# Weight conversion spread over the feed-forward part of two batches, the first quarter of w_in converted by columns, and first scores kept in PSUM

## The chip, the cores and the metric

The kernel runs on one core of a Trainium2 chip. The metric is the device time of one execution in microseconds. The kernel before takes 824.21 us (median of three runs, 824.08 to 826.26).

## What is computed

For each of 8 batches and 8 heads, 32 packed queries p attend to 576 keys and values of width 64; the result is both key and value for a second attention, by 576 queries q. The 8 heads side by side are the 512 inputs of a feed-forward layer (FFN) with 2048 hidden units and a leaky rectifier.

```python
def sm_attn(qq, kk, vv):
    s = scale * np.matmul(qq, kk.transpose(0, 1, 3, 2))
    s = s - np.max(s, axis=-1, keepdims=True)
    a = np.exp(s)
    a = a / (np.sum(a, axis=-1, keepdims=True) + 1e-09)
    return np.matmul(a, vv)
p_packed = sm_attn(p, k, v)
x = sm_attn(q, p_packed, p_packed)
h = x @ w_in
g = np.maximum(h, 0.0) + alpha * np.minimum(h, 0.0)
out = g @ w_out
```

## The kernel before

**Engines and numbers.** Matmuls in full precision are done in one of two ways. Either both operands are split into a high and a low part and three fast matmuls are summed (hi*hi, hi*lo, lo*hi), or plain f32 operands are used; such a matmul is two instructions in the trace. The weights w_in and w_out arrive as 64-bit floats, and the kernel itself turns them into f32, 128 rows by 512 columns at a time, in `convert` (L103 to L134): a 512 KB load on SP's queue (L112), two ACT instructions (L117, L119), four DVE instructions (L120, L123, L127, L131), then a split into high part (ACT L133) and low part (DVE L134). There are 16 such pieces of w_out and 16 of w_in, 32 **conversions**. The raw data go into buffers that later hold converted w_out pieces (`new_raw`; four of them are kept in turn, `SPARE = 4`).

**Attention.** `attention(b, tp)` treats two of the four head pairs of a batch: scores of the packed queries (`scores`, L189), softmax (L259 to L268), transposes (L294), the packed values (L311 or L316), scores of q (L362, L364), a transpose on DVE (L367), softmax by POOL and DVE over groups of 32 (L369 to L378), and a last transpose into the FFN's input: `a_f` in f32 for batch 0 (L383), `a_h` and `a_l` for the others (L390 to L392). For batches 0 and 1 scores are plain f32 matmuls with 64 output rows (L200), which ACT and DVE copy from PSUM to SBUF (L202, L204).

**Packed weights.** `packed_w` multiplies each piece of w_in with the packed values of a batch (L435 to L437) and so yields `pw`, the FFN's first weights in packed form; on the first use (`fresh`) it converts the piece and writes it split to DRAM (`w_split`, L407); later uses read it back.

**FFN.** The tokens of batch b are the halves k = 2b and 2b+1, of 288 columns each. `first(k, f)` makes 128 hidden units (L468 for batch 0: four instructions; L480 to L482 for the others: six), then ACT L486, DVE L487, ACT L492, DVE L493 make the rectified value, split. `second(k, f)` adds it to four output blocks (L505 to L507: twelve matmuls). One pair (k, f) is an **iteration**; there are 256, the ACT row of L486 marks each one's start, and second runs two iterations behind first. For batch 1 and later `split_pw` first splits pw: high part on DVE (L456), low part on POOL for batch 1 and on DVE from batch 2 on (L458). `order` takes batch 0 in quarters of f, both halves in turn, so that four partial sums are added (`part`, L511, L518); the other batches have all 16 f of one half in a row.

**What sets the order.** `plan` (L574 to L582) says at which iteration which generator (conversions `wo`, `w0`; attention of later batches; packed weights) makes a step, and how often. All w_in pieces for batch 0 (`w0`) and all w_out pieces (`wo`) are converted at one step every second iteration, after a prologue `PRO` of ten steps. A list scheduler then orders each engine's instructions; an engine runs its own list strictly in order, so an instruction that waits holds all behind it, and SP's queue of DMA issues does too.

Of the kernel before, what the change touches and what calls it, by code (L numbers as in the profile page):

```python
# [28 lines left out]
def pack_attention_ffn_kernel(  # L29
# [50 lines left out]

    w_split = dram.tile([NJ, NP, P, 2, 512], F32, name="w_split")


    ident = const.tile([P, P], F32, name="ident")
    make_identity(nc, ident)
    ii = const.tile([P, 64], F32, name="ii")
    nc.gpsimd.tensor_copy(out=ii[0:64], in_=ident[0:64, 0:64])
    nc.gpsimd.tensor_copy(out=ii[64:128], in_=ident[64:128, 64:128])
# [5 lines left out]
    s1f = const.tile([P, NP, 64], F32, name="s1f")  # L94
    p2f = const.tile([P, NP, 64], F32, name="p2f")
    pt0 = const.tile([P, NP, 2, 2, 64], F32R, name="pt0", tag=f"wo{NF - 1}")
    for t in (s1f, p2f, fv(s1), fv(p2), fv(pt0)):
        nc.gpsimd.memset(t, 0.0)
    wo_t = {}

    XF = 1

    def convert(src, raw, place):  # L103
# [8 lines left out]
        nc.sync.dma_start(out=raw, in_=src)  # L112
# [6 lines left out]
        nc.scalar.activation(out=low, in_=u[:, :, 0], func=AF.Copy, scale=2.0**-29)  # L119
        nc.vector.tensor_scalar(  # L120
# [9 lines left out]
        )  # L130
        nc.vector.tensor_tensor(out=bits, in0=bits, in1=low, op=ALU.add)  # L131
# [16 lines left out]
    SPARE = 4  # L148
    left = list(range(NF - 1 - SPARE, NF - 1))

    def load_w_out(f):
# [4 lines left out]
        raw = new_raw(f)  # L156
        convert(w_out[f * P : (f + 1) * P, :], raw, place)
# [31 lines left out]
    def scores(b, pr, st, x, dst, exact):  # L189

        ro = (pr % 2) * 64
        for hf in range(2):
            sl = slice(hf * HS, hf * HS + HS)
            if exact:
                if b == 0:
                    tag = f"acc{(2 * pr + hf) % 4}"
                    ps = ps_a.tile([P, 512], F32, name=tag, tag=tag)
                else:
                    ps = ps_m.tile([P, 512], F32, name="ps_m", tag="m")
                nc.tensor.matmul(ps[:64, :HS], st[:, pr], x[:, sl], start=True, stop=True)  # L200
                if hf or b > 0:
                    nc.scalar.copy(out=dst[ro : ro + 64, sl], in_=ps[0:64, :HS])  # L202
                else:
# [3 lines left out]
            nc.tensor.matmul(ps[:, :HS], st[:, pr], x[0][:, sl], start=True, stop=False)  # L207
# [426 lines left out]
```

## Time and profile before

| | |
|---|---|
| median of three runs | 824.21 us |
| profiled execution, its time | 824.1 us |
| its span, first to last instruction | 822.0 us |
| busy: PE / DVE / ACT / POOL | 782.6 / 607.2 / 486.6 / 206.6 us |
| mean granted clock | 0.985 |

A page of the profile gives the busy time of each engine; the span cut in 40 slices shows it in tenths. Matmuls overlap, so that a PE shown as busy may still be waiting between matmuls; how much it does is told by the number of matmuls in a stretch, and by how long a run of them takes when nothing waits. The timeline gives start and length of single instructions, and the table by stretch gives busy time and, in brackets, the number of instructions.

### The profile page before, as it was taken

How to read it: one execution, taken by the hardware profiler on the slowest of the kernel's cores; microseconds unless marked ns; L12 is line 12 of the kernel's file. 1: busy time of each engine (PE TensorE's matmuls, PEld its weight loads, DVE VectorE, ACT ScalarE, POOL GpSimd, SP SyncE). 2: the span in 40 equal slices, each digit the busy share in tenths (PEclk: the TensorE clock that was granted, in tenths of full speed). 3: DMA queues.
4: the chain of work that ended last, by engine and by line, in shares of the span. 5: the costliest groups of instructions: out<-in, count | busy, mean ns of one | idle time of the engine just before them, and what ended most of it. 6: DMA issues, size and time to landing. Idle time of an engine off the chain costs nothing.

```text
span 822.0 us, 14951 instructions
## 1 busy us (share of the span) xinstructions
PE 782.6 (95%) x5384; PEld 729.1 (89%) x5384; DVE 607.2 (74%) x1303; ACT 486.6 (59%) x1141; POOL 206.6 (25%) x203
## 2 busy tenths in 40 slices
PE   5679998999999999999999999999999999999997
PEld 3357686898799999999999999899999999999997
DVE  4999898975777557899886488987855566666663
ACT  5778866766666775656667765665655533333332
POOL 2100022536667401353362024533210000000000
PEclk9769999999999999999999999999999999999999
DMA  9777855664633561321227621300262000000000
GB/s 301 261 247 234 271 189 197 200 197 160 211 91 109 188 229 44 92 72 60 62 83 237 206 84 52 104 24 15 81 206 84 23 30 2 30 1 30 1 31 29
DMA packets 55385, 97.96 MB, mean 119 GB/s; under 512 B 5136, under 2 KB 32784, under 8 KB 55312
## 3 DMA queue, kind: packets, MB, share of 16 engines
q1 hardware_dynamic: 55312, 97.02, 36.3%
q8 instruction: 42, 0.69, 0.4%
q14 instruction: 31, 0.25, 0.1%
HBM read 79.18 MB, written 17.83 MB: 118 GB/s over the span
## 4 chain that ended last, share of the span: by engine, by line
PE 75%; DVE 13%; ACT 5%; DMA 4%; issue 2%; SPq 1%; POOL 0%; ACTq 0%; DVEq 0%
PE acc L505 15%; PE acc L506 14%; PE acc L507 14%; PE ps_h L480 7%; PE ps_h L482 7%; PE ps_h L481 7%; PE ps_m L435 2%; PE ps_m L436 2%; PE ps_m L437 2%; DMA wraw<-in_w_out 2%; PE ps_h L468 1%; PE ps_m L316 1%; DVE ps_h L487 1%; DVE pwl L458 1%; DVE mag L127 1%
## 5 line engine op out<-in xcount | busy, mean ns | idle before, releaser
L505 PE MATMUL acc<-gh,wo 128*128 128x288 f32 x1024 | 286.8, 300 | 6.8 <-ACT gh L492 4.9
L506 PE MATMUL acc<-gh,wo 128*128 128x288 f32 x1024 | 281.5, 294 | 0.0
L505 PEld LDWEIGHTS acc<-gh,wo 128*128 128x128 f32 x1024 | 192.2, 188 | 18.0 <-ACT gh L492 10.5
L507 PE MATMUL acc<-gl,wo 128*128 128x288 f32 x1024 | 201.0, 301 | 0.0
L506 PEld LDWEIGHTS acc<-gh,wo 128*128 128x128 f32 x1024 | 192.3, 188 | 1.4
L492 ACT CAST gh<-ps_h 128x288 fp32r<-128x288 f32 x256 | 102.2, 399 | 122.0 <-DVE ps_h L487 120.0
L493 DVE TENSOR_TENSOR gl<-ps_h,gh 128x288 fp32r<-128x288 f32 x256 | 115.5, 452 | 73.9 <-ACT gh L492 72.4
L486 ACT ACTIVATE neg<-ps_h 128x288 f32<-128x288 f32 x256 | 105.4, 412 | 104.8 <-PE ps_h L482 98.8
L507 PEld LDWEIGHTS acc<-gl,wo 128*128 128x128 f32 x1024 | 157.8, 188 | 3.6
L487 DVE SCALAR_TENSOR_TENSOR ps_h<-neg,nal,ps_h 128x288 f32<-128x288 f32 x256 | 131.4, 515 | 35.2 <-ACT neg L486 34.2
L480 PE MATMUL ps_h<-a_h,pwh 128*128 128x288 f32 x448 | 133.2, 297 | 1.0 <-DVE gl L493 0.9
L482 PE MATMUL ps_h<-a_h,pwl 128*128 128x288 f32 x448 | 132.1, 296 | 0.7 <-POOL pwl L458 0.7
L481 PE MATMUL ps_h<-a_l,pwh 128*128 128x288 f32 x448 | 131.9, 295 | 0.0
L173 POOL TENSOR_TENSOR xl<-xraw,xh 128x576 fp32r<-128x576 f32 x48 | 70.1, 1461 | 134.4 <-ACT xh L172 124.6
L480 PEld LDWEIGHTS ps_h<-a_h,pwh 128*128 128x128 f32 x448 | 84.1, 188 | 2.9 <-DVE gl L493 1.9
L482 PEld LDWEIGHTS ps_h<-a_h,pwl 128*128 128x128 f32 x448 | 83.9, 188 | 1.3 <-POOL pwl L458 1.1
L481 PEld LDWEIGHTS ps_h<-a_l,pwh 128*128 128x128 f32 x448 | 84.1, 188 | 0.5
L456 DVE CAST pwh<-pw 128x512 fp32r<-128x512 f32 x112 | 55.3, 496 | 35.2 <-PE ps_h L481 33.3
L458 DVE TENSOR_TENSOR pwl<-pw,pwh 128x512 fp32r<-128x512 f32 x96 | 74.7, 778 | 6.6 <-PE ps_h L482 0.8
L443 ACT COPY pw<-ps_m 64x512 f32<-64x512 f32 x112 | 65.0, 581 | 19.2 <-PE ps_m L437 15.3
L275 POOL TENSOR_TENSOR vs<-vraw,vs 128x640 fp32r<-128x640 f32 x24 | 38.6, 1608 | 42.4 <-ACT vs L274 42.4
L210 ACT COPY lo<-ps_m 64x288 f32<-64x288 f32 x96 | 37.8, 395 | 16.9 <-PE ps_m L208 15.4
(112 smaller groups left out, 1021.7 us busy)
## 6 DMA issues: line engine op xcount, KB each, us to landing
w<-w_split SPq DMA_DIRECT2D x64, 512.0 KB, 3.9
xraw<-in_kT SPq DMA_DIRECT2D x32, 288.0 KB, 2.9
xraw<-in_qT SPq DMA_DIRECT2D x32, 288.0 KB, 3.1
outT<-ot SPq DMA_DIRECT2D x64, 144.0 KB, 1.9
vraw<-in_v SPq DMA_DIRECT2D x32, 256.0 KB, 2.9
wraw<-in_w_out SPq DMA_DIRECT2D x16, 512.0 KB, 4.2
wraw<-in_w_in SPq DMA_DIRECT2D x16, 512.0 KB, 5.0
w_split<-w SPq DMA_DIRECT2D x16, 512.0 KB, 4.8
```

The costliest lines, as they stand in the source:

```text
L173: nc.gpsimd.tensor_tensor(out=xl, in0=raw, in1=fv(xh), op=ALU.subtract)
L458: eng.tensor_tensor(out=tl, in0=src, in1=fv(th), op=ALU.subtract)
L480: nc.tensor.matmul(ps[:, :HS], th[:, i, fs], a_h[:, i, tok], start=hi, stop=False)
L481: nc.tensor.matmul(ps[:, :HS], th[:, i, fs], a_l[:, i, tok], start=False, stop=False)
L482: nc.tensor.matmul(ps[:, :HS], tl[:, i, fs], a_h[:, i, tok], start=False, stop=lo)
L486: nc.scalar.activation(out=neg, in_=g, func=AF.Relu, scale=-1.0)
L487: nc.vector.scalar_tensor_tensor(out=g, in0=neg, scalar=nal[:, f : f + 1], in1=g, op0=ALU.mult, op1=ALU.add)
L492: nc.scalar.copy(out=gh, in_=g)
L493: nc.vector.tensor_tensor(out=gl, in0=g, in1=fv(gh), op=ALU.subtract)
L505: nc.tensor.matmul(acc[o][:, :HS], wo_t[f][:, 0, os_], gh, start=begin, stop=False)
L506: nc.tensor.matmul(acc[o][:, :HS], wo_t[f][:, 1, os_], gh, start=False, stop=False)
L507: nc.tensor.matmul(acc[o][:, :HS], wo_t[f][:, 0, os_], gl, start=False, stop=end)
```

## The change

- **Order.** Batch 0's FFN still has four quarters, but batch 1's is cut in two (`SWEEPS`), and the two batches take turns: quarters 1 and 2 of batch 0, first half of batch 1, quarters 3 and 4 of batch 0, second half of batch 1. Partial sums of batch 1 come new; `part` moves to the pool of pw.
- **First quarter of w_in.** `packed_w_fine` converts it in four pieces of 128 columns of all four head pairs, so that one piece serves one f; piece and packed values stay plain f32. The second quarter comes by 128 rows in f32 (`packed_w_first`). Both write w_whole (f32, half of w_split's bytes) to DRAM. For batch 1 these two quarters are read back from w_whole and split (ACT L573, DVE L574) and then written to w_split; the last two quarters are converted once for both batches (`packed_w([0, 1], ..., "fresh")`).
- **Scores of batch 0** have 128 output rows: the operand has zeros where the other pair's rows are, two matmuls add up in one PSUM tile, and maximum, exponential and DVE transpose read PSUM. The copies L202 and L204 are gone for batch 0.
- **Engines.** Batch 0's two group-softmax steps go from POOL to DVE (L432, L439). Batch 1's pw split goes to ACT (high) and DVE (low, L616). The packed values' split for batches 0 and 1 goes from ACT and DVE to POOL (`split_pt`).
- Raw buffers: `SPARE` 6 for 4. The steps A2 and AG of later attention are set later.

Core of the diff (`convert` also yields between its parts and can write f32 by `whole`):

```diff
-    SPARE = 4
+    SPARE = 6
...
-                nc.tensor.matmul(ps[:64, :HS], st[:, pr], x[:, sl], start=True, stop=True)
-                if hf or b > 0:
-                    nc.scalar.copy(out=dst[ro : ro + 64, sl], in_=ps[0:64, :HS])
-                else:
-                    nc.vector.tensor_copy(out=dst[ro : ro + 64, sl], in_=ps[0:64, :HS])
+                    nc.tensor.matmul(
+                        dst[hf][:, :HS], st, x[:, sl], start=(pr % 2 == 0), stop=(pr % 2 == 1)
+                    )
...
+        if whole is not None:
+            nc.vector.tensor_tensor(out=whole().bitcast(U32), in0=bits, in1=low, op=ALU.add)
+            return
...
-        eng = nc.vector if b < 0 else nc.gpsimd
+        eng = nc.vector if b < 1 else nc.gpsimd
...
+    def packed_w_fine(j):
+        def get(f):
+            cols = slice((4 * j + f) * P, (4 * j + f) * P + P)
+            w = new_w32()
+            raw = new_raw()
+            steps = convert(
+                w_in.rearrange("(r p) c -> p r c", p=P)[:, :, cols],
+                raw, None, lambda: w, raw.rearrange("p (r c) -> p r c", r=NP),
+            )
+            drain(steps)
+            nc.sync.dma_start(
+                out=w_whole[j].rearrange("r p c -> p r c")[:, :, f * P : f * P + P],
+                in_=w.rearrange("p (r c) -> p r c", r=NP),
+            )
+            return w
...
+                nc.tensor.matmul(
+                    ps[:, t : t + P], pt0[:, pr].rearrange("d s n -> d (s n)"),
+                    ws[f][:, pr * P : pr * P + P], start=(pr % 2 == 0), stop=(pr % 2 == 1),
+                )
...
+    def packed_w(bs, units, source="split"):
+        def get(j, pr):
+            w = win.tile([P, 2, 512], F32R, name="w", tag="w")
+            if source == "split":
+                nc.sync.dma_start(out=fv(w), in_=w_split[j, pr])
+                return w
+            if source == "whole":
+                raw = xin.tile([P, 512], F32, name="w32", tag="xraw")
+                nc.sync.dma_start(out=raw, in_=w_whole[j, pr])
+                nc.scalar.copy(out=w[:, 0, :], in_=raw)
+                nc.vector.tensor_tensor(
+                    out=w[:, 1, :], in0=raw, in1=fv(w[:, 0, :]), op=ALU.subtract
+                )
+            else:
+                drain(convert_w_in(j, pr, lambda: (w[:, 0, :], w[:, 1, :])))
+            nc.sync.dma_start(out=w_split[j, pr], in_=fv(w))
+            return w
...
-        nc.vector.tensor_copy(out=th, in_=src)
-        eng = nc.gpsimd if k < 4 else nc.vector
-        eng.tensor_tensor(out=tl, in0=src, in1=fv(th), op=ALU.subtract)
+        if k < 4:
+            nc.scalar.copy(out=th, in_=src)
+        else:
+            nc.vector.tensor_copy(out=th, in_=src)
+        nc.vector.tensor_tensor(out=tl, in0=src, in1=fv(th), op=ALU.subtract)
...
-    order = [(h, 4 * j + f) for j in range(NJ) for h in range(2) for f in range(4)]
-    order += [(k, f) for k in range(2, 2 * B) for f in range(NF)]
+    SWEEPS = [(0, 4, 8, 12), (0, 8)] + [(0,)] * (B - 2)
...
+    order = sweep(0, 0) + sweep(0, 4) + sweep(1, 0) + sweep(0, 8) + sweep(0, 12) + sweep(1, 8)
...
-    PRO = "oPPwoPwPoo"
-    for ch in PRO:
-        next(wo if ch == "o" else w0)
+    for ch in "zzzzzzzzPzzzPzzzzoozzzP":
+        next({"z": z, "P": wf, "o": wo}[ch], None)
...
-    A1 = (-1, 6, 19)
-    A2 = (17, 20, 30, 34, 40)
-    AG = (-8, -5, 12, 15, 30)
-    E = 2
-    plan = [(0, w0, E), (0, wo, E)]
...
+    WO, W1, AT1 = (-7, 5, 4), 2, (-1, 2, -3)
+    PW1, PW01, PW01B = (7, -2), (13, 3), (25, -8)
+    A2 = (24, 29, 34, 38, 53)
+    AG = (0, 5, 10, 17, 30)
+    plan = [(0, wf, 1), (WO[0], slower(WO[1], WO[2], wo), 1), (W1, packed_w_first(1), 1)]
...
```

**How lists move.** First place: SP's queue at the start of the program, which issues all loads. Before, the first raw weights (wraw) stand behind all keys, values and queries of batch 0:

```order
L182 DMA vraw_160<-in_v 128x4x128
L186 DMA vraw_160<-in_v 64x128
L166 DMA xraw<-in_qT 128x576 x2
L182 DMA vraw_199<-in_v 128x4x128
L186 DMA vraw_199<-in_v 64x128
L182 DMA vraw_218<-in_v 128x4x128
L186 DMA vraw_218<-in_v 64x128
L166 DMA xraw<-in_qT 128x576
L166 DMA xraw_258<-in_qT 128x576
L112 DMA wraw_320<-in_w_out 128x512
```

Of the change:

```order
L189 DMA vraw_168<-in_v 128x4x128
L193 DMA vraw_168<-in_v 64x128
L189 DMA vraw_174<-in_v 128x4x128
L193 DMA vraw_174<-in_v 64x128
L115 DMA wraw_179<-in_w_in 128x4x128
L173 DMA xraw<-in_qT 128x576 x2
L189 DMA vraw_233<-in_v 128x4x128
```

The first raw weights now stand ahead of all four loads of queries and of the last pair's values.

Second place: DVE just ahead of the last input of the FFN, the second transpose into a_f. Before (mag and low are the conversion's):

```order
L134 TENSOR_TENSOR w<-mag,w 128x512
L123 TENSOR_SCALAR mag<-mag 128x512 x2
L377 RECIPROCAL z_314<-z_314 128x18
L127 SCALAR_TENSOR_TENSOR mag<-wraw_415,mag 128x512
L127 SCALAR_TENSOR_TENSOR mag<-wraw_433,mag 128x512
L120 TENSOR_SCALAR mag<-mag 128x512
L131 ISA mag<-mag,low 128x1024 x2
L383 STREAM_TRANSPOSE a_f<-t_308 128x576
```

Of the change:

```order
L438 RECIPROCAL z_374<-z_374 128x18
L299 TENSOR_SCALAR den<-den 128x1
L132 SCALAR_TENSOR_TENSOR mag<-wraw_491,mag 128x512
L142 TENSOR_TENSOR wo_432<-mag,wo_432 128x512
L439 TENSOR_TENSOR t_348<-t_348,z_374 128x576
L300 RECIPROCAL den<-den 128x1
L137 ISA w_490<-mag,low 128x1024
L142 TENSOR_TENSOR wo_478<-mag,wo_478 128x512
L444 STREAM_TRANSPOSE a_f<-t_348 128x576
```

In both lists the transpose stands behind conversions: eight of them are done ahead of it before, nine in the change; the step on POOL between reciprocal and transpose (L378) has become DVE's L439.

Third place: DVE at the 13th to 15th iteration. Before:

```order
L487 SCALAR_TENSOR_TENSOR ps_h<-neg,nal,ps_h 128x288
L263 TENSOR_SCALAR den<-den 128x1
L131 ISA mag<-mag,low 128x1024
L493 TENSOR_TENSOR gl<-ps_h,gh 128x288
```

Of the change (w_966 and the like are pieces read back from w_whole):

```order
L647 SCALAR_TENSOR_TENSOR ps_h<-neg,nal,ps_h 128x288
L430 TENSOR_REDUCE m_851<-t_849 128x18
L139 ISA mag<-mag,low 128x1024
L574 TENSOR_TENSOR w<-w_966,w 128x512
L574 TENSOR_TENSOR w<-w_987,w 128x512
L574 TENSOR_TENSOR w<-w_1015,w 128x512
L436 TENSOR_REDUCE z_871<-t_849 128x18
L437 TENSOR_SCALAR z_871<-z_871 128x18
L438 RECIPROCAL z_871<-z_871 128x18
L653 TENSOR_TENSOR gl<-ps_h,gh 128x288 x2
```

Three splits, each of which waits for a load, for ACT, and for a free buffer w (of three), now stand between an iteration's L647 and its L653, which second waits for.

## Rows read from the trace of the kernel before

**Rows 1.** Page: the span, and PE's busy tenths in 40 slices.
```profile
span 822.0 us, 14951 instructions
...
PE   5679998999999999999999999999999999999997
```

**Rows 2.** Table by stretch: length, then busy us and (instructions) per engine, clock, DMA.
```profile
0.00:53.00 53.00, 31.00 (x113) 17.94 (x114) 39.98 (x81) 32.82 (x73) 9.52 (x23) 0.78 0.80 268
53.00:150.30 97.30, 93.32 (x503) 72.08 (x502) 91.16 (x195) 73.35 (x169) 13.74 (x14) 0.99 0.69 231
150.30:288.20 137.90, 133.75 (x915) 123.67 (x914) 97.47 (x224) 94.71 (x219) 78.48 (x70) 1.00 0.50 161
288.20:822.00 533.80, 524.50 (x3858) 515.40 (x3856) 378.60 (x805) 285.69 (x683) 104.86 (x97) 1.00 0.23 73
```

**Rows 3.** Table by stretch, L486 alone: ACT busy and (instructions), that is iterations begun.
```profile
53.00:150.30 97.30, 9.85 (x24) 0.99 0.69 231
150.30:288.20 137.90, 16.43 (x40) 1.00 0.50 161
```

**Rows 4.** Table by stretch, L127 alone: DVE busy and (instructions), that is conversions.
```profile
17.00:53.00 36.00, 6.90 (x9) 0.68 0.77 259
...
53.00:150.30 97.30, 15.46 (x22) 0.99 0.69 231
150.30:288.20 137.90, 0.68 (x1) 1.00 0.50 161
```

**Rows 5.** PE's groups from 53 to 288.2 us: count, busy, mean ns, idle before.
```profile
L505 PE MATMUL acc<-gh,wo 128*128 128x288 f32 x252 | 72.8, 308 | 3.4 <-ACT gh L492 2.4 <-ACT part L511 0.7
...
L468 PE MATMUL ps_h<-a_f,pw 128*128 128x288 f32 x122 | 36.3, 420 | 0.8 <-DVE gl L493 0.8
L480 PE MATMUL ps_h<-a_h,pwh 128*128 128x288 f32 x66 | 19.7, 300 | 0.1
...
L435 PE MATMUL ps_m<-w,pt 128*128 128x512 f32 x21 | 8.7, 415 | 0.2 <-ACT w L133 0.2
```

**Rows 6.** Chain that ended last: start, length, what; runs of matmuls without a wait.
```profile
156.87 0.97 PE ps_h L468 x4
...
291.12 0.54 PE acc L507 x4
291.65 0.23 PE ps_m L435
```

**Rows 7.** DVE's timeline: start, length, instruction.
```profile
17.33 0.43 DVE L120 TENSOR_SCALAR mag<-mag 128x512 f32<-128x512 f32 x1 [2.64 <-ACT mag L117]
...
34.63 0.68 DVE L131 CUSTOM_DVE_ANT_0 mag<-mag,low 128x1024 uint16<-128x1024 uint16 x1
...
36.91 1.65 DVE L131 CUSTOM_DVE_ANT_0 mag<-mag,low 128x1024 uint16<-128x1024 uint16 x1
...
49.11 0.77 DVE L383 STREAM_TRANSPOSE a_f<-t 128x576 f32<-128x576 f32 x1
```

**Rows 8.** POOL's timeline at the same time.
```profile
36.80 1.20 POOL L371 TENSOR_TENSOR t<-t,m 128x576 f32<-128x576 f32 x1 [7.13 <-DVE m L369]
```

**Rows 9.** Chain: the load of the first raw weights; ACT's timeline: the first iteration.
```profile
10.78 5.83 DMA wraw<-in_w_out
...
52.96 0.41 ACT L486 ACTIVATE neg<-ps_h 128x288 f32<-128x288 f32 x1 [0.26 <-PE ps_h L468]
```

**Rows 10.** DVE's groups of the whole execution: count, busy, mean ns.
```profile
L131 DVE CUSTOM_DVE_ANT_0 mag<-mag,low 128x1024 uint16<-128x1024 uint16 x32 | 22.5, 709 | 0.0
...
L134 DVE TENSOR_TENSOR w<-mag,w 128x512 fp32r<-128x512 f32 x16 | 10.8, 673 | 0.6 <-ACT w L133 0.6
```

**Rows 11.** Page, DMA issues: KB each, median us from issue to landing.
```profile
vraw<-in_v SPq DMA_DIRECT2D x32, 256.0 KB, 2.9
...
w_split<-w SPq DMA_DIRECT2D x16, 512.0 KB, 4.8
```

**Rows 12.** SP's queue: who it waited for, us in total, times, longest.
```profile
SPq L112 <- DVE mag L127: 33.0, 17, 6.0
```

More of the change, by code (lines that the diff above doesn't have):

```diff
@@ L101, in pack_attention_ffn_kernel, with convert @@
     XF = 1
-    def convert(src, raw, place):
-        nc.sync.dma_start(out=raw, in_=src)
+    def convert(src, raw, place, whole=None, room=None):
+        nc.sync.dma_start(out=raw if room is None else room, in_=src)
+        yield
         u = raw.bitcast(U32).rearrange("p (f t) -> p f t", t=2)
@@ L119, in convert @@
         nc.scalar.activation(out=low, in_=u[:, :, 0], func=AF.Copy, scale=2.0**-29)
+        yield
         nc.vector.tensor_scalar(
@@ L240, in attention @@
                 if exact:
-                    nc.scalar.copy(out=s1f[rs, :, cs], in_=praw[rs])
+                    for i in range(2):
+                        nc.scalar.copy(out=s1f[rs, i::2, i, cs], in_=praw[rs, i::2])
                 else:
@@ L385, in attention @@
             )
+            done.add(("a", b, tp))
+            yield
+            split_pt()
             return
@@ L392, in attention, with new_pw, ahead @@
         nc.gpsimd.tensor_tensor(out=a_l[:, tp, :], in0=s2, in1=fv(a_h[:, tp, :]), op=ALU.subtract)
+        done.add(("a", b, tp))
         yield
[L396 to L411 removed]
+    def new_pw(bs, j):
+        for b in bs:
+            pw[b, j] = pwp.tile([P, 2, 512], F32, name="pw", tag="pw")
+    def ahead(get, units):
         ws = []
@@ L446, in packed_w, with packed_w_whole @@
+            yield None
+        for n, u in enumerate(units):
+            yield u, ws[n]
             if n + LA < len(units):
                 ws.append(get(*units[n + LA]))
+    def packed_w_whole(j, ws):
+        new_pw([0], j)
+        for pr in range(NP):
+            if pr % 2 == 0:
+                ps = ps_m.tile([P, 512], F32, name="ps_m", tag="m")
+            st = pt0[:, pr].rearrange("d s n -> d (s n)")
+            assert ("p", 0, pr) in done
+            done.add(("w", 0, j, pr))
+            nc.tensor.matmul(ps, st, ws[pr], start=(pr % 2 == 0), stop=(pr % 2 == 1))
+            if pr % 2:
+                nc.scalar.copy(out=pw[0, j][:, pr // 2, :], in_=ps)
+            yield
@@ new lines, in packed_w_first @@
+    def packed_w_first(j):
+        ws = []
+        for pr in range(NP):
+            w = new_w32()
+            drain(convert_w_in(j, pr, None, lambda: w))
+            nc.sync.dma_start(out=w_whole[j, pr], in_=w)
+            ws.append(w)
+            if pr < 2:
+                yield
+                continue
+            if pr == 2:
+                gen = packed_w_whole(j, ws)
+                next(gen)
+                next(gen)
+                yield
+                continue
+            next(gen)
+            next(gen)
+            yield
@@ L462, in first @@
         tok = slice((k % 2) * HS, (k % 2) * HS + HS)
+        assert all(("a", k // 2, tp) in done for tp in range(2)), ("a", k)
+        assert k < 2 and ("wf", f) in done or all(("w", k // 2, f // 4, pr) in done for pr in range(4)), ("w", k, f)
         ps = ps_h.tile([P, 512], F32, name="ps_h", tag="h")
@@ L547, in after, with slower @@
         yield from gen
+    def slower(n, m, gen):
+        for i, _ in enumerate(gen):
+            yield
+            if i + 1 >= n:
+                for _ in range(m - 1):
+                    yield
     def zipped(*gens):
```

271 lines of the change are left out of this document (169 added, 102 removed).

## Prediction

> **What bounds the kernel now.** I began with the page's slices [rows 1]: PE is under nine tenths only in the first three of 40, so that some 20 us seem to be all there is to win. The table by stretch [rows 2], cut where iterations 1, 25 and 65 begin [rows 3, 9], shows more, and three different limits. Up to 53.0 us no iteration begins: PE executes 113 instructions at a mean clock of 0.78, while DVE is busy for 40.0. From 53.0 to 150.3 us 24 iterations run; DVE is busy for 91.2 of 97.3 us, because 22 of the 32 conversions fall there [rows 4], and PE issues 503 matmuls. From 150.3 to 288.2 us 40 iterations run with one conversion; DVE is busy for 97.5 of 137.9. The remaining 192 iterations take 533.8 us with 3858 matmuls, one per 0.138 us, which is close to the 0.135 of a run without a wait [rows 6].
>
> How full is PE really? PE's busy time says 95% and hides the answer, since matmuls overlap. I count instead. A fast 288-column matmul costs 0.54 / 4 = 0.135 us, an f32 instruction 0.97 / 4 = 0.243, a 512-column one 0.23 [rows 6]. Between 53 and 288.2 us [rows 5] there are 3 x 252 (L505 to L507, alike) + 3 x 66 (L480 to L482, alike) + 64 of the attention = 1018 of the first kind, 137.4 us; 122 of L468 and 30 of L200 in f32, 36.9; 112 with 512 columns (three lines of 21 or 22 with full rows, 48 with half), 25.8; and 134 short ones of 64 to 256 columns, 14.3 by columns. That is **214.4 us of matmul work in 235.2, 20.8 lost**. With the 53 us in front and about 14 lost in the last stretch, these are the places from which the change can take.
>
> **The change, part by part.** The sum has four terms: when the first iteration begins, the matmul work of 64 iterations, what is lost in them, and the rest.
>
> *First iteration.* Before, DVE starts its first conversion step at 17.33 us, when the first raw weights have landed, and reaches the FFN's last input, the second a_f, at 49.11 [rows 7]: 31.8 us of nearly unbroken work. The weights were issued at 10.78 us behind all of batch 0's loads and took 5.83 [rows 9]; in the change they stand ahead of five loads with their parts, so I put the landing some 4 us earlier, at 13. DVE's list up to a_f then holds nine conversions instead of eight, but only four with the last subtraction instead of six: + 1 x (0.7 + 0.7 + 0.4), L127 taken as long as L131 [rows 10] and L123 as L120 [rows 7], - 2 x 0.67 (L134 [rows 10]) = +0.5. The four PSUM copies L204 of 288 columns and four small splits go, -2.1 by columns against L134's 512 in 0.67, an estimate. Batch 1's first maximum and some small ones come, +1.3. The four group-softmax steps come from POOL to DVE. No row shows them on DVE; L134 with 512 columns takes 0.67 [rows 10], which with 576 is 0.75, an estimate; bounds are 0.45 and 1.0; so +3.0. In exchange, four collisions go: while POOL runs L371 for 1.20 us [rows 8], DVE's L131 that starts with it takes 1.65 instead of 0.68 [rows 7]; 4 x 0.95 = -3.8. Together -1.1: the list is as long as before, and only its start moves. 13 + 30.7 = 43.7 for a_f; I add 1.5 since the list may now run ahead of batch 0's attention, and 2.5 for the last matmul, ACT's L486 and a low clock: before, it was 3.8 from 49.11 to 52.96 [rows 9], with one more weight product between. **First iteration at 47.5 us**, between 43 (nothing waits) and 53 (the loads are no earlier, as DMA moves 268 GB/s there already [rows 2]).
>
> The Trainium skill, SBUF — State Buffer, section Who interferes with whom, says that a DVE instruction with two SBUF inputs and a POOL instruction that reads SBUF exclude each other for the whole instruction. The pair L131 and L371 agrees: 1.65 is 0.68 plus nearly a POOL step. By that rule all 20 large POOL steps taken away (4 here, 16 of L458 for batch 1) give back about 1 us each of DVE time, and the sum would be lower by at most what the second stretch has lost, about 7 us. I count only the four: in the second stretch DVE has 40 us to spare [rows 2].
>
> *Work of 64 iterations.* The change packs two quarters of w_in for both batches at once and uses plain f32 for two quarters of batch 0. Its list holds, between its first and 65th iteration, 1024 fast matmuls of 288 columns (138.2 us), 152 f32 instructions (36.9), 66 with 512 columns (15.2), four f32 products with 512 columns (eight instructions, 3.5 by columns, an estimate) and the same short ones (14.2): **208.0 us**, 6.4 less. Half of this is work that has moved ahead of the first iteration; a true saving is about 3.7.
>
> *Lost in them.* This is the uncertain term. The name of the change says that conversions spread; the list says how far: 11 stand ahead of the first iteration, 18 in iterations 1 to 24, 3 after, against 9, 22 and 1 [rows 4]. So DVE loses four conversions of some 2.5 us in the first 24 iterations, but gains up to eight splits L574 of 0.6 and a batch 1 attention that comes earlier; I put its list 3 us shorter. At the ratio of length to DVE's list as before, the stretch would take 94 us, and I add 1 for waits on buffers w (third rival): 95 for 97.3. PE's work in it is 85 us, so 10 are lost. In the next 40 iterations DVE gets 16 low splits of 0.6 from POOL and three conversions; its load rises from 0.71 [rows 2] to about 0.75, no bound. What was late at batch 1's start was the chain from packed weights by ACT, DVE and POOL; in the change it is one engine shorter and its pieces come earlier. PE's work there is 123 us; I take 4.5 lost for 7 before. **14.5 lost** instead of 20.8; bounds 5 (PE only) and 23 (as before, and two more waits).
>
> *Nothing elsewhere.* Scores with 128 rows instead of 64 take as many columns, so PE's price is the same; the ACT and DVE copies they save are in the first term. Partial sums of batch 1 add eight ACT copies of 0.3 and eight DVE additions in place of as many copies, hidden under ACT's 0.69 busy share in the second stretch [rows 2]; without that cover they'd cost 5 us. w_whole adds 4 MB of traffic to some 60 moved in these stretches, at a DMA share of 0.5 to 0.8. The short pieces cost nothing in the rows: loads of 256 KB in 512-byte runs (vraw) land in 2.9 us [rows 11]. Six raw buffers instead of four shorten SP's waits for DVE's L127, 33.0 us in total, longest 6.0 [rows 12]; next late is then DVE itself. The rest, 533.8 us [rows 2], keeps its instructions; attention is started some iterations later, -3 to +4, taken as 0.
>
> *Sum.* 47.5 + 208.0 + 14.5 + 533.8 = 803.8 us of span; the profiled run has 2.1 us around its span (824.1 for 822.0): **806 us**, against 824.1 for that run, which stands 0.1 under the median of 824.21.
>
> **The rivals.**
> *The front opens fully* (0.17). Nothing in the list waits, loads land at 12 us, PE alone bounds from the first iteration: 43 + 208 + 5 + 531 + 2 = 789. For it: DVE's load in iterations 25 to 64 is 0.75. Against: 18 conversions still fall in the first 24, where DVE's list and PE's work are both near 85 us.
>
> *It doesn't spread* (0.15). DVE's lists up to the first iteration are equally long and early loads do not help because DMA is the limit: 53 + 208 + 21 + 534 + 2 = 818. For it: the counts 9, 22, 1 against 11, 18, 3. Against: early loads come ahead of others that are needed later, and collisions with POOL do go.
>
> *Read-backs block DVE* (0.10): slower. Eight L574 stand in DVE's list ahead of L653, on which PE's second waits, and each needs one of three buffers w, free only when the store to w_split of three pieces earlier has landed, 4.8 us [rows 11]. If the pieces go one by one, DVE stands still for up to 4.8 us at all but the first two: 6 x 4.8 = 29 us, 806 + 29 = 835. It decides from 18 / 6 = 3 us of wait per piece. Against: three buffers in turn make it one third of that, and five iterations lie between first and last piece.
> The Trainium skill, DMA: Bandwidth & Descriptors, section on the anatomy of one DMA, says that a DMA's semaphore wait is held by the issuing sequencer, not by the DMA engines; a store to w_split that waits for DVE thus holds the loads behind it. SP's waits for DVE agree [rows 12]. By that rule this case is likelier than the buffers alone make it; since no row of before shows a read-back behind such a store, I leave it at one in ten.
>
> **How the numbers follow.** Forecast 0.55, the three rivals 0.17, 0.15 and 0.10, and 0.03 for mishaps. The forecast's own range is 797 to 815: first term 44 to 51, lost 8 to 20, rest -3 to +4, not all at one end. The range of 790 to 820 takes in most of the first rival and of the second and leaves out the third. A measurement of this kernel can tell about 0.3% from no change, 821.7 to 826.7 us. Faster: forecast, first rival, nearly all of the second, 0.86. Within: 0.04. Slower: the third rival, 0.10.
>
> **What would show it.** The first L646 of ACT (before L486) at about 47 us, and wraw landing near 13; DVE's t steps at about 0.75 us without collisions. From first to 25th iteration about 95 us, with DVE over 0.9 busy; from there to the 65th about 127 instead of 137.9, PE issuing a matmul per 0.14 us. Wrong would be a first iteration later than 51 us, a DVE waiting at L574 for more than 2 us at a time, PE waiting for L653 in iterations 12 to 18, or a last stretch of more than 540 us.

## The result, and the profile after

The changed kernel takes **813.46 us** (median of four runs, 811.3 to 815.2) against 824.68 of the kernel before beside it: ratio 0.986, interval 0.984 to 0.988. A second set of runs gave 812.4 and 0.986 (0.983 to 0.988). The forecast was 806 in a range of 790 to 820: faster, by 11 us instead of 18. The profiled execution, the shortest of the first four, takes 811.3 us, 2.0 more than its span. Page of the change, as [rows 1]:

```profile
span 809.3 us, 14930 instructions
...
PE   6779899999989899999999999999999999999997
```

The table by stretch, cut at iterations 1, 25 and 65, as [rows 2]:

```profile
0.00:49.10 49.10, 31.44 (x142) 22.95 (x143) 35.19 (x84) 32.62 (x80) 7.82 (x27) 0.89 0.90 307
49.10:147.50 98.40, 93.79 (x532) 74.55 (x531) 91.68 (x184) 84.17 (x185) 20.79 (x20) 0.99 0.77 255
147.50:277.30 129.80, 124.68 (x862) 117.89 (x861) 101.40 (x234) 92.33 (x218) 53.28 (x52) 1.00 0.33 99
277.30:809.30 532.00, 523.12 (x3847) 514.14 (x3845) 377.55 (x802) 287.98 (x685) 109.50 (x97) 1.00 0.24 77
```

Where the 12.7 us of span come from is read off against [rows 2]: the first iteration starts 3.9 us earlier (49.1 for 53.0). The 24 iterations after it take 1.1 us *longer* (98.4 for 97.3). The next 40 are 8.1 shorter (129.8 for 137.9), and the rest is 1.8 shorter. The two middle stretches together take 228.2 us instead of 235.2. With the 208.0 us of matmul work that the prediction counted in the list, 20.2 are lost in them. Counted in the trace, as before was, the work between the same two iterations is 209 us (1036 fast matmuls with 288 columns, 145 f32 instructions, 71 with 512 columns, 8 f32 with 512, and the short ones), and 19 are lost, against 20.8 before. So the change gave less work, an earlier start and a small gain in the rest; **it took at most 2 us off what PE loses in these 64 iterations**.

In iterations 1 to 24 the loss has no single owner. What PE waited for there, the three longest (engine, line waited for: us in total, times, longest):

```profile
PE acc L670 <- ACT gh L652: 1.8, 2, 1.0
PE ps_m L212 <- ACT ptf L383: 1.6, 1, 1.6
PE ps_h L628 <- DVE gl L653: 0.6, 1, 0.6
```

L212 (scores of q against batch 1's packed values ptf) waits for ACT to copy them (L383). ACT's timeline shows what stands ahead of that copy:

```profile
87.21 0.72 ACT L310 CAST vs<-vraw 128x640 fp32r<-128x640 f32 x1 [1.41 <-DMA vraw<-in_v]
87.84 0.39 ACT L652 CAST gh<-ps_h 128x288 fp32r<-128x288 f32 x1
88.13 0.41 ACT L646 ACTIVATE neg<-ps_h 128x288 f32<-128x288 f32 x1
88.83 0.68 ACT L121 ACTIVATE mag<-wraw 128x512 f32<-128x512 f32 x1 [0.29 <-DMA wraw<-in_w_out]
89.40 0.67 ACT L123 ACTIVATE low<-wraw 128x512 uint32<-128x512 uint32 x1
89.98 0.66 ACT L455 CAST a_h<-s 128x576 fp32r<-128x576 f32 x1
90.54 0.67 ACT L123 ACTIVATE low<-wraw 128x512 uint32<-128x512 uint32 x1
91.11 0.42 ACT L383 COPY ptf<-ps_m 64x64 f32<-64x64 f32 x2
```

A cast of batch 2's values, not due for 16 iterations, waits for its load; conversion steps follow; the copy that PE waits for comes after them.

### The profile page after: what moved, and what is told of

It is laid out like the page before. It is cut to its first block, busy times and chain, and to the rows that moved or that the text cites. A ratio compares the mean times of both kernels' runs of the same rounds, so it can differ in the third digit from the quotient of the medians.

```text
span 809.3 us, 14930 instructions
## 1 busy us (share of the span) xinstructions
PE 773.0 (96%) x5376; PEld 729.5 (90%) x5376; DVE 605.8 (75%) x1301; ACT 497.1 (61%) x1165; POOL 191.4 (24%) x195
## 4 chain that ended last, share of the span: by engine, by line
PE 80%; DVE 8%; DMA 5%; ACT 5%; issue 1%; POOL 0%; SPq 0%; ACTq 0%; DVEq 0%
PE acc L670 15%; PE acc L671 15%; PE acc L672 15%; PE ps_h L640 7%; PE ps_h L641 7%; PE ps_h L642 7%; PE ps_h L628 3%; DMA vraw<-in_v 2%; PE ps_m L352 2%; PE ps_m L216 1%; PE ps_m L217 1%; PE ps_m L596 1%; PE ps_m L598 1%; PE ps_m L597 1%; DMA w<-w_split 1%
## 5 line engine op out<-in xcount | busy, mean ns | idle before, releaser
L652 ACT CAST gh<-ps_h 128x288 fp32r<-128x288 f32 x256 | 101.6, 399 | 115.3 <-DVE ps_h L647 113.2
L646 ACT ACTIVATE neg<-ps_h 128x288 f32<-128x288 f32 x256 | 105.3, 412 | 107.2 <-PE ps_h L642 95.5
L653 DVE TENSOR_TENSOR gl<-ps_h,gh 128x288 fp32r<-128x288 f32 x256 | 115.2, 452 | 70.4 <-ACT gh L652 68.5
L647 DVE SCALAR_TENSOR_TENSOR ps_h<-neg,nal,ps_h 128x288 f32<-128x288 f32 x256 | 131.2, 515 | 47.2 <-ACT neg L646 46.5
L640 PE MATMUL ps_h<-a_h,pwh 128*128 128x288 f32 x448 | 134.2, 300 | 4.1 <-DVE gl L653 4.0
L616 DVE TENSOR_TENSOR pwl<-pw,pwh 128x512 fp32r<-128x512 f32 x112 | 83.7, 748 | 9.1 <-ACT pwh L613 3.5
L640 PEld LDWEIGHTS ps_h<-a_h,pwh 128*128 128x128 f32 x448 | 84.2, 188 | 6.1 <-DVE gl L653 5.3
L601 ACT COPY pw<-ps_m 64x512 f32<-64x512 f32 x120 | 69.6, 580 | 15.2 <-PE ps_m L598 12.5
L615 DVE CAST pwh<-pw 128x512 fp32r<-128x512 f32 x96 | 52.0, 542 | 28.6 <-PE ps_h L641 27.8
L311 POOL TENSOR_TENSOR vs<-vraw,vs 128x640 fp32r<-128x640 f32 x24 | 40.4, 1682 | 51.3 <-ACT vs L310 50.3
L628 PE MATMUL ps_h<-a_f,pw 128*128 128x288 f32 x128 | 39.6, 433 | 3.8 <-DVE a_f L444 3.0
```

The lines of the kernel that those rows point to most:

```text
L616: nc.vector.tensor_tensor(out=tl, in0=src, in1=fv(th), op=ALU.subtract)
L640: nc.tensor.matmul(ps[:, :HS], th[:, i, fs], a_h[:, i, tok], start=hi, stop=False)
L646: nc.scalar.activation(out=neg, in_=x, func=AF.Relu, scale=-1.0)
L647: nc.vector.scalar_tensor_tensor(out=x, in0=neg, scalar=nal[:, f : f + 1], in1=x, op0=ALU.mult, op1=ALU.add)
L652: nc.scalar.copy(out=gh, in_=x)
L653: nc.vector.tensor_tensor(out=gl, in0=x, in1=fv(gh), op=ALU.subtract)
```

## The experiments

All thirteen runs (twelve kernels) in one table. The stretches, in us, are cut where each execution's own iterations 1, 25 and 65 begin. "Spells" is the time after 56 us and ahead of the end in which the profile shows TensorE at a granted clock of 0.5 (1.2 instead of 2.4 GHz). Stretches and spells are those of the one profiled execution of each row. Medians are of 4 to 10 runs; before stood at 824.1 to 825.3 beside them.

| kernel | median us | ratio to before (interval) | first iteration | 1 to 24 | 25 to 64 | rest | spells |
|---|---|---|---|---|---|---|---|
| the change | 813.46 | 0.986 (0.984-0.988) | 49.1 | 98.3 | 129.9 | 532.0 | 0 |
| after_again | 812.40 | 0.986 (0.983-0.988) | 47.5 | 99.4 | 131.3 | 531.9 | 3.4 |
| one_later | 820.26 | 0.996 (0.994-0.998) | 50.4 | 102.5 | 133.6 | 536.2 | 10.2 |
| no_clamp | 821.32 | 0.995 (0.993-0.997) | 47.7 | 102.2 | 130.7 | 535.5 | 10.2 |
| small_clamp | 821.13 | 0.996 (0.994-0.998) | 47.0 | 104.2 | 132.7 | 533.6 | 6.8 |
| rows_first | 820.35 | 0.995 (0.993-0.997) | 51.8 | 101.6 | 129.9 | 535.2 | 3.4 |
| scores_copied | 822.92 | 0.998 (0.996-1.000) | 54.7 | 98.8 | 131.5 | 535.0 | 3.4 |
| in_turn_undone | 826.61 | 1.002 (1.000-1.003) | 49.2 | 109.8 | 129.1 | 537.0 | 17.1 |
| pool_back | 819.27 | 0.993 (0.991-0.995) | 50.2 | 102.3 | 131.3 | 533.8 | 13.6 |
| pwl_pool | 825.01 | 1.000 (0.998-1.001) | 50.0 | 101.8 | 134.9 | 538.1 | 17.1 |
| ahead3 | 827.69 | 1.006 (1.001-1.011) | 47.5 | 105.8 | 130.7 | 541.8 | 6.8 |
| vs_on_pool | 821.87 | 0.997 (0.994-0.999) | 49.0 | 97.8 | 135.8 | 533.6 | 3.4 |
| pw1_late | 819.12 | 0.992 (0.990-0.995) | 49.9 | 100.3 | 131.6 | 535.4 | 6.8 |

**First set: is DVE's list the bound, and what are three parts worth?** The theory was the prediction's: the length of the 24 iterations follows DVE's list.

no_clamp:

```diff
-        nc.vector.tensor_scalar(
-            out=mag, in0=mag, scalar1=F64_BOTTOM, scalar2=F64_TOP, op0=ALU.max, op1=ALU.min
-        )
```

> The changed kernel without the first DVE step of each conversion (L125, the clamp of magnitudes; 0.335 us from start to start, 32 times): it leaves out the limits for very small and very large weights. Theory 'DVE's list bounds up to the 25th iteration': 11 of them stand ahead of the first iteration, 3.7 us, and 18 in the first 24 iterations, 6.0 us, so the first iteration comes at 45 to 46.5 us for 49.1, the next 24 take 92 to 94 for 98.4, and the time falls by 7 to 10 us to 803 to 806. Rival 'PE's own work and the chain of one iteration bound': the first stretch keeps 97 us or more and the time falls by less than 3 us. Rival 'loads bound the start': the first iteration stays at 48.5 or later.

DVE's busy time in the stretch falls from 91.7 to 85.5 us, as asked, and the stretch takes 102.2 us instead of the 92 to 94 expected. That it is longer than the change's 98.3 shows nothing: it holds a spell of 6.8 us at the lower clock, worth some 3 us (priced under pw1_late), and the same lists alone gave 98.3 to 102.5 (one_later, below). Without the instruction the list scheduler orders everything anew, so a cleaner edit followed later (small_clamp).

rows_first (the first quarter of w_in by 128 rows, as the second):

```diff
-    wf = packed_w_fine(0)
+    wf = packed_w_first(0)
```

> The first quarter of w_in by 128 rows of one head pair at a time (as the second quarter), all else as changed. Theory 'DVE's list': all four column pieces stand ahead of the last a_f in DVE's list, as four row pieces will, so the columns bring nothing that counts: time within 2 us of 813. Rival 'the first piece by columns is what lets the FFN begin': the first iteration comes 3 to 6 us later, at 52 to 55, and the time is 816 to 819.

scores_copied (batch 0's scores with 64 output rows and PSUM copies, as before):

```diff
-                    nc.tensor.matmul(
-                        dst[hf][:, :HS], st, x[:, sl], start=(pr % 2 == 0), stop=(pr % 2 == 1)
-                    )
-                    continue
...
+                if hf or b > 0:
+                    nc.scalar.copy(out=dst[ro : ro + 64, sl], in_=ps[0:64, :HS])
+                else:
+                    nc.vector.tensor_copy(out=dst[ro : ro + 64, sl], in_=ps[0:64, :HS])
```

> Batch 0's scores with 64 rows and copied from PSUM by ACT and DVE as before, all else as changed. Theory 'DVE's list': eight copies more of 0.37 us on DVE and eight on ACT, less four small reductions and two split transposes, make the list ahead of the first iteration 1 to 2 us longer, and the first conversions are not earlier: first iteration at 50 to 52, time 814 to 816. Rival 'the chain of batch 0's attention sets the start': each pair's chain grows by copy and wait, 4 us, first iteration at 53, time 817. Rival 'DVE waits for loads up to 21 us anyhow': no difference.

in_turn_undone:

```diff
-    order = sweep(0, 0) + sweep(0, 4) + sweep(1, 0) + sweep(0, 8) + sweep(0, 12) + sweep(1, 8)
+    order = sweep(0, 0) + sweep(0, 4) + sweep(0, 8) + sweep(0, 12) + sweep(1, 0)
...
-    WO, W1, AT1 = (-7, 5, 4), 2, (-1, 2, -3)
-    PW1, PW01, PW01B = (7, -2), (13, 3), (25, -8)
+    WO, W1, AT1 = (-7, 5, 2), 2, (-1, 2, -3)
+    PW1, PW01, PW01B = (20, -2), (7, -2), (13, 1)
```

> Batch 0's four quarters first, then batch 1 whole, as before; the last two quarters of w_in still converted once for both batches and so ahead of iterations 17 and 25; w_out at every second step instead of every fourth. Theory 'taking turns is what keeps conversions out of the first 24 iterations': more than 22 conversions there instead of 18, DVE full, the stretch takes 106 to 112 us instead of 98.4, the next one gains less than that back: 817 to 822. Rival 'the gain of the second stretch is from packing two batches at once and from splitting on one engine less': within 2 us of 813.

Here 23 conversions (L132) run in iterations 1 to 24, and the stretch takes 109.8 us, in the 106 to 112 of the first theory; but spells of 13.6 us lie in it too, worth some 6 of the 11.5 us.

All three kernels are slower than the dearest case expected for them, by 1 us (rows_first, beyond 819), 6 (scores_copied, beyond 817) and 5 (in_turn_undone, beyond 822). Each of the three undone parts costs 7 to 13 us, 30 together, and the whole change gains 11. They do not add up: either the parts need each other, or something else is in each price. The first iteration of scores_copied is 5.6 us later than the change's, more than the spread between executions of the same lists (47.5 to 50.4, below). So the start is really later; whether by the copies themselves or by the lists that were ordered anew around them is not separated. For rows_first (2.7 us later) even the delay is only probable.

**Second set: execution to execution, DVE once more, POOL, and more slack.** after_again is the change itself.

> The changed kernel once more, beside the next three on one chip. Its four executions so far had spans of 809.3, 810.6, 813.3 and 812.4 us at mean granted clocks of 0.992, 0.989, 0.987 and 0.986. If that spread is the clock's alone, the iterations begin again at about 49 (first), 147.5 (25th) and 277.4 us (65th), and every stretch that comes out longer holds one more spell at a granted clock of 0.5. If waits differ from execution to execution, stretches differ without such a spell.

The lists are identical, and still the first iteration comes at 47.5 instead of 49.1; one spell of 3.4 us appears in the 25 to 64. one_later and pw1_late (below) have the same lists up to there too, and give 50.4 and 49.9: the first term alone spreads by 3 us. The repeat also has a stop of 2.08 us at L596, near 280 us, that is 1.48 in the first execution.

small_clamp:

```diff
-            out=mag, in0=mag, scalar1=F64_BOTTOM, scalar2=F64_TOP, op0=ALU.max, op1=ALU.min
+            out=mag[:, :8], in0=mag[:, :8], scalar1=F64_BOTTOM, scalar2=F64_TOP, op0=ALU.max, op1=ALU.min
```

> The clamp at L125 works on 8 of 512 columns, so that large values in the weights' 64-bit form are no longer clamped in the other 504; the instruction stays in DVE's list, which stands far nearer to that of the change than without it. Each conversion gets some 0.28 us shorter on DVE (0.335 in the trace with 512 columns). If DVE's list bounds the start and iterations 1 to 24: first iteration 9 x 0.28 = 2.5 us earlier, at 46.6, and the stretch of 24 iterations 18 x 0.28 = 5 us shorter, 93 instead of 98.4; 7.5 us in all. If the lists of PE, ACT and DVE hold each other up in turn and no single one bounds: the first iteration comes 1 to 2.5 us earlier, but the stretch stays at 97 to 100 us.

The small clamps take a median of 164 ns instead of 0.4 us, the first iteration comes at 47.0, and the 24 iterations take 104.2 us, a spell of 6.8 among them (table by stretch):

```profile
47.05:151.29 104.24, 97.25 (x534) 76.36 (x533) 90.22 (x184) 86.62 (x188) 18.69 (x20) 0.95 0.72 250
```

DVE's sum falls by only 1.5 us here, so this run is a weak test. With no_clamp it speaks against DVE as the one bound, not for another one.

pool_back:

```diff
-        eng = nc.vector if b < 1 else nc.gpsimd
+        eng = nc.gpsimd
```

> Batch 0's two group-softmax steps go back from DVE to POOL, four instructions. By the prediction's prices DVE's list up to the first iteration loses 4 x 0.75 = 3.0 us and gets 4 collisions of 0.95 = 3.8: first iteration at 49 to 50.5, all later stretches as in the change. Rival: the steps stand in the chain of batch 0's attention, and on POOL each takes 1.20 instead of 0.75 with a change of engine on both sides; then the first iteration comes 1.5 to 4 us later, at 50.6 to 53. Against both: if the move was worth nothing because POOL's time was hidden, it stays at 49.1 within 0.3.

50.2 lies inside the 47.5 to 50.4 that identical lists gave: nothing is shown of the move's worth at the start. In the profiled execution it costs 8 us (5.8 by the medians), and 13.6 us at half clock are worth some 6 of them (how a spell is priced is shown under pw1_late). PE's stop at L212 before the first spell is 2.6 us here, 1.6 in the change.

ahead3:

```diff
-    AHEAD = 2
+    AHEAD = 3
```

> Second runs three iterations behind first instead of two, with four buffers gh and gl instead of three (and two output buffers instead of four, for room). In the trace of the change PE's visible waits in iterations 1 to 24 are for gh at L670 (1.8 us), for the packed queries at L212 (1.6) and for a free ps_h at L628 and L640 (0.9). If the loss in the 64 iterations is the wait of second for its rectified value behind DVE's and ACT's lists: iterations 1 to 24 get 2 to 4 us shorter, 25 to 64 by 1 to 2. If each wait that goes is replaced by the next one in the lists' order: 98.4 and 129.8 within 1.5 us.

The edit also takes four buffers gh and gl for three and, for room, two output buffers for four. The slowest kernel of all, against both expectations: the waits for gh do not go (2.2 us in iterations 1 to 24), packed weights become late (L596 waits 3.3 us for ACT's L601 there), and the rest is 10 us longer. How much of that is due to the two output buffers was not tested.

**Third set: take the visible stop away.** vs_on_pool:

```diff
-            nc.scalar.copy(out=vs[:, :, 0, :], in_=vraw[i])
+            if b == 2:
+                nc.gpsimd.tensor_copy(out=vs[:, :, 0, :], in_=vraw[i])
+            else:
+                nc.scalar.copy(out=vs[:, :, 0, :], in_=vraw[i])
```

> The cast of batch 2's values (L310) goes from ACT to POOL, four instructions. In the trace of the change the first of them stands in ACT's list at 87.2 us, 16 iterations before batch 2's attention is due; ACT waits there 1.4 us for its load, and behind it stand a neg, batch 1's packed queries ptf (L383) and gh; PE then waits 1.6 us at L212 for ptf, its longest wait in iterations 1 to 24. If a load that is late under a full DMA, and an in-order ACT behind it, make that loss: the 24 iterations get 1.5 to 3 us shorter than 98.4 to 99.4, the clock stays at 1.00 there, 25 to 64 stay. If ACT's list is simply full there (mag and low of two conversions follow): the wait at L212 stays at 1 us or more and the stretch within 1 us. If moved instructions reorder the lists for the worse: PE stops for over 2.5 us somewhere in iterations 4 to 12, a spell at granted clock 0.5 follows, and the stretch takes over 101 us.

The wait at L212 falls from 1.6 to 1.1 us and the stretch to 97.8, half a microsecond below the change's. That is the second of the expected cases: ACT's list is simply full there. The gain is lost in 25 to 64 (135.8), where other stops appear: 1.9 us at first's f32 matmul (L628 of the change), followed by a spell.

pw1_late:

```diff
-    PW1, PW01, PW01B = (7, -2), (13, 3), (25, -8)
+    PW1, PW01, PW01B = (10, -2), (13, 3), (25, -8)
```

> Batch 1's read-back of the first two quarters of w_in begins at iteration 10 instead of 7, nothing else. It takes eight loads, eight casts L573 (0.62 us each on ACT) and eight splits L574 out of the place where batch 1's attention, a conversion and a full DMA already meet (80 to 95 us). If that meeting makes the loss in iterations 1 to 24: iterations 5 to 12 get 2 to 4 us shorter, and 0 to 2 us come back between iterations 12 and 20, where the splits now fall together with first of batch 1; in all 1 to 3 us faster than the change. If every wait is replaced by another: within 1.5 us. Against: the weights of batch 1 come too late for its first iteration (the 17th); then PE waits at L640 for more than 3 us, a spell at granted clock 0.5 follows, and the run is 4 to 8 us slower than the change.

The kernel is 5.7 us slower than the change. The wait for ptf is gone, and a longer one came later, not at L640 for late weights but for gh. PE's timeline:

```profile
120.88 0.40 PE L598 MATMUL ps_m<-w,pt 128*128 128x512 f32 x1
125.62 0.40 PE L670 MATMUL acc<-gh,wo 128*128 128x288 f32 x1 [4.34 <-ACT gh L652]
125.86 0.29 PE L671 MATMUL acc<-gh,wo 128*128 128x288 f32 x1
125.99 0.38 PE L670 MATMUL acc<-gh,wo 128*128 128x288 f32 x1
126.17 0.44 PE L671 MATMUL acc<-gh,wo 128*128 128x288 f32 x1
126.41 0.44 PE L670 MATMUL acc<-gh,wo 128*128 128x288 f32 x1
126.65 0.44 PE L671 MATMUL acc<-gh,wo 128*128 128x288 f32 x1
```

DVE has finished ps_h for that gh (L647) at 121.64 us. ACT makes neg for it (L646) at 120.36 and gh (L652) only at 125.17; between them it executes eight other instructions of its list without a gap. After the stop the second and third matmul start 0.13 us apart, from the fourth on it is 0.24: the granted clock has fallen to 0.5, and a spell costs a little under half its length.

pwl_pool:

```diff
-        if k < 4:
-            nc.scalar.copy(out=th, in_=src)
-        else:
-            nc.vector.tensor_copy(out=th, in_=src)
-        nc.vector.tensor_tensor(out=tl, in0=src, in1=fv(th), op=ALU.subtract)
+        nc.vector.tensor_copy(out=th, in_=src)
+        eng = nc.gpsimd if k < 4 else nc.vector
+        eng.tensor_tensor(out=tl, in0=src, in1=fv(th), op=ALU.subtract)
```

> The split of batch 1's pw goes back to its engines before: high part on DVE, low part on POOL (eight pairs of instructions). DVE exchanges eight subtractions of 0.6 us for eight copies, POOL gets eight steps of over 1 us, and batch 1's chain from pw by the split to its first matmuls crosses one engine more. If this part of the change carried nothing of the gain: 25th to 65th iteration within 1 us of 129.9 to 131.3, total within 2 us of the change. By the prediction's words (one engine shorter): the start of batch 1's halves waits 1 to 2 us longer, twice or four times, 2 to 5 us in all. The rule on shared input gives some 8 us of DVE time blocked by POOL; DVE has 35 us to spare in that stretch, so that at most 2 us of it shows.

12 us slower, far over every price named (there are sixteen such pairs, not eight as expected). Its 25 to 64 are 5 us longer, but the rest, where none of them stands, is 6 longer. That cannot be the price of the pairs alone.

**Fourth: the order alone.** one_later:

```diff
-    A2 = (24, 29, 34, 38, 53)
+    A2 = (25, 29, 34, 38, 53)
```

> Batch 2's attention is due at iteration 25 instead of 24; work, engines, buffers and loads are the change's, and the lists of all engines are the same row by row up to about iteration 20 to 24, different after it. It prices nothing but the order of the lists. If the 7 to 13 us that each undone part cost were the prices of the parts, this costs 0 within 1.5 us: 129.9 to 131.3 us from the 25th to the 65th iteration and 532 after. If they were for the larger part the price of any other order than the one that the change has: the stretch from the 25th to the 65th and the rest get 2 to 8 us longer together, with a stop of PE of 2 us or more that the change does not have, or the change's own stops (2.0 us at L640 near 229 us, 1.5 at L596 near 278) longer and followed by a spell at granted clock 0.5. The first 24 iterations stay at 98 to 99.5 us by both.

The same work, one due time moved by one iteration, and **7 us are gone** (820.26 against 813.46 and 812.40). 25 to 64 and the rest are 8 us longer together in the profiled execution (one of its longest, 824.67), with a stop of 2.5 us at L596, where the change's two executions have 1.5 and 2.1, and a spell after it that they do not have there. By the traces, all engines' lists are the change's up to 142 us. Even so the first 24 iterations did not stay in the expected 98 to 99.5: they took 102.5. So this stretch spreads from 98.3 to 102.5 between executions of the same lists, and the 101.6 to 102.3 of rows_first, no_clamp, pool_back and pwl_pool are no prices of their edits. What differs is the stop at L212 again. PE in the change:

```profile
88.77 1.24 PE L628 MATMUL ps_h<-a_f,pw 128*128 128x288 f32 x4
91.58 1.18 PE L212 MATMUL ps_m<-xraw,ptf 128*64 128x288 f32 x4 [1.57 <-ACT ptf L383]
```

and in one_later, then its table by stretch there:

```profile
90.66 1.24 PE L628 MATMUL ps_h<-a_f,pw 128*128 128x288 f32 x4
94.13 1.32 PE L212 MATMUL ps_m<-xraw,ptf 128*64 128x288 f32 x4 [2.23 <-ACT ptf L383]
```

```profile
92.00:94.00 2.00, 0.00 (x0) 0.00 (x0) 1.69 (x4) 1.99 (x6) 0.72 (x1) 1.00 0.70 227
94.00:96.00 2.00, 1.37 (x5) 0.51 (x5) 2.00 (x3) 1.98 (x6) 1.92 (x3) 0.76 0.04 12
96.00:98.00 2.00, 2.00 (x4) 1.12 (x4) 1.89 (x4) 0.77 (x3) 0.22 (x1) 0.50 0.61 182
```

The same list and a wait of 2.23 us instead of 1.57: ACT stood for two loads ahead of it (1.46 and 0.99 us, in the change 1.41 and 0.29), and the granted clock falls to 0.5 for 6.8 us. At some 0.45 of its length that is 3 of the 4.2 us by which the stretch is longer. The 7 us between the medians are another matter: whatever the new order costs must lie after 142 us.

Not tried were four raw buffers instead of six, and the splits L574 on POOL.

## Why the prediction was right, and where it was not

- **First iteration, 47.5: right within the spread.** 49.1, and 47.5 in the repeat. The raw weights' first step stands at 12.99 (forecast: landing near 13), the group-softmax step on DVE takes 0.75 (forecast 0.75), and a_f comes at 46.95 (45.2). DVE's timeline, as [rows 7]:

```profile
12.99 0.41 DVE L125 TENSOR_SCALAR mag<-mag 128x512 f32<-128x512 f32 x1
...
17.43 0.43 DVE L125 TENSOR_SCALAR mag<-mag 128x512 f32<-128x512 f32 x1 [1.56 <-ACT mag L121]
...
21.61 0.43 DVE L125 TENSOR_SCALAR mag<-mag 128x512 f32<-128x512 f32 x1 [1.74 <-ACT mag L121]
...
45.02 0.75 DVE L439 TENSOR_TENSOR t<-t,z 128x576 f32<-128x576 f32 x1
...
46.95 0.77 DVE L444 STREAM_TRANSPOSE a_f<-t 128x576 f32<-128x576 f32 x1
```

  The sum's list of 30.7 us was right as a whole: 12.99, 30.7 and the two gaps, 3.3 us, give the 46.95. For such gaps, the list running ahead of batch 0's attention, the sum held 1.5 (its terms make 47.7, put down as 47.5): before both, ACT comes to the conversion's step L121 only after steps of that attention. The scores' copies and four small splits were priced at 2.1 us; with the copies back the first iteration is 4 to 7 later. That suggests that the chain of batch 0's attention is nearer to the bound than DVE's sum said.
- **Work, 208.0, 6.4 less than before: right.** The trace has 209, between 5 and 6 less. This is the largest part of the gain; a part of it, as the prediction says, is work that now stands ahead of the first iteration (142 instructions of PE there instead of 113).
- **Lost in 64 iterations, 14.5: the step that failed**; it measured 19 to 20. The words were "I put its list 3 us shorter. At the ratio of length to DVE's list as before, the stretch would take 94 us". The list is 0.5 us longer (91.68 for 91.16 [rows 2]). First, conversions were counted by their place in the list, 18 for iterations 1 to 24; in time DVE lags behind, and it is 20, as [rows 4]:

```profile
12.00:49.10 37.10, 6.23 (x9) 0.85 0.92 321
49.10:147.50 98.40, 13.81 (x20) 0.99 0.77 255
147.50:277.30 129.80, 2.04 (x3) 1.00 0.33 99
```

  Four conversions fewer, 10 us, became two fewer; with three that need no last subtraction, DVE's conversion steps take 56.5 us there for 64.8, added up without regard to overlaps. Second, more came in. DVE's groups, before in its 24 iterations and then the change's:

```profile
L131 DVE CUSTOM_DVE_ANT_0 mag<-mag,low 128x1024 uint16<-128x1024 uint16 x22 | 14.8, 678 | 0.0
```

```profile
L139 DVE CUSTOM_DVE_ANT_0 mag<-mag,low 128x1024 uint16<-128x1024 uint16 x17 | 13.9, 823 | 0.2
...
L574 DVE TENSOR_TENSOR w<-w,w 128x512 fp32r<-128x512 f32 x8 | 6.4, 800 | 1.8 <-ACT w L573 1.7
...
L616 DVE TENSOR_TENSOR pwl<-pw,pwh 128x512 fp32r<-128x512 f32 x6 | 4.0, 685 | 0.2 <-ACT pwh L613 0.2
```

  The splits L574 take 0.8 us each instead of the 0.6 put for them. Six of batch 1's sixteen low splits L616 fall here, 4.0 us; the prediction put all sixteen into the next 40 iterations. L139 is dearer, 823 ns for 678, with POOL busy for 20.8 us instead of 13.7 [rows 2]; a conversion as a whole is not (2.8 us for 2.9).

  Third, the ratio itself does not hold: with 6 us less of DVE the stretch did not get shorter (no_clamp). PE, ACT and DVE are busy for 94, 84 and 92 of 98 us, each in a fixed order. Where an edit took away the wait at L212 (pw1_late) or a part of it (vs_on_pool), longer ones came later. What does set the length of the stretch was not found.
- **25 to 64, 127.5: 129.8, and 2.3 us is about the length of one stop.** The chain that ended last, there:

```profile
227.89 0.28 DVE s L256
...
228.21 1.51 DVE s L256
...
230.31 0.47 DVE gl L653
...
230.82 0.40 PE ps_h L640
```

  and POOL's timeline beside it:

```profile
228.17 1.41 POOL L456 TENSOR_TENSOR a_l<-s,a_h 128x576 fp32r<-128x576 f32 x1 [1.85 <-ACT a_h L455]
```

  A 64 x 128 subtraction takes 0.28 us, and 1.51 beside POOL's 1.41; first's next matmul stood for 2.04 us behind it. The Trainium skill, SBUF — State Buffer, section Who interferes with whom, has the rule (the two exclude each other), and these rows agree. The prediction counted the collisions that go at the start and none that come: nothing in its sum held POOL's other steps against DVE's new places. Over the whole execution, L139 takes 1.00 us on average in the 8 of 24 cases in which POOL's work overlaps it by over 0.2 us, and 0.68 in the others.
- **Rest, 533.8: 532.0**, inside -3 to +4. **Around the span 2.1: 2.0.**
- **The rivals.** "It doesn't spread" was nearly right on the spread (9, 20 and 3 conversions, against 9, 22 and 1 before) and on the loss (21, for 19 to 20), and wrong on the start (53, for 49.1); the result lies between it and the forecast. "The front opens fully" fell: the two stretches lost nearly as much as before. "Read-backs block DVE" fell: DVE waits at L574 for 1.7 us in all, 1.4 at most, and for ACT; ACT's L573, which writes the buffer w first, waits for 2.1 us in all, for the load from w_whole and not for a free buffer.

**What stays open.** The waits that the profile shows add up to 4.5 us in iterations 1 to 24 and 4.9 in 25 to 64; the other half of the loss shows in no wait there, and no run here took it apart (about 1 us is the clock of 0.5 that lasts until 51.7 us). That the change's order is a favourable one is suggested by its neighbours: all eleven other kernels are 6 to 14 us slower. But only one_later does the same work, and it is a single other order. Why the change's order stops PE less was not found, and so the parts' own prices stay open.

## What to carry to other kernels

Count the matmul work and the time when the first matmul can start; these two terms held. Do not price a stretch by the sum of one engine's list when three engines are over 0.85 busy in a fixed order, and count operations by when they run, not by where they stand. Before you call the difference of two kernels the price of an edit, run a neutral one that only shifts the order: here that alone was worth 7 us, as much as rows_first and more than pool_back. And before you read one stretch of one execution as a price, look how far it spreads with the same lists: here by 3 us at the start and by 4 in the 24 iterations after it.

## What the runs showed of the hardware that was not expected

The granted clock falls in the middle of a kernel whose PE is 95% busy. In these kernels there are 23 spells at 0.5 after 56 us, of 3.4 or 6.8 us each; each begins within 5 us of the beginning of a stop of PE. The stops ahead of them last from 1.0 us (two short ones at 281.6 and 283.5 us in in_turn_undone) to 4.3 us (pw1_late). A stop does not decide it alone: first's L640 waited 2.04 us at 228.8 in the change without a spell, and 2.05 at 228.2 in the repeat with one; the repeat's 2.08 at L596 had none. The same program differs by some us from execution to execution, in part with the clock: the change's four runs have spans of 809.3, 810.6, 813.3 and 812.4 us at mean clocks of 0.992, 0.989, 0.987 and 0.986. The kernel before has no spell after 56 us, and its longest stop there is 1.16 us.
